# Block-sparse attention and a top-1 expert router on one core: a third of the score mask moves from TensorE to GpSimd, settled rows are divided later, ranks are kept in 16 bits, and 25 expert tiles always run

## The chip, the cores and the metric

The kernel runs on one core of one Trainium2 chip, and the metric is the device time of one execution in microseconds (us). The engines are PE (TensorE, matrix multiply; its weight loads are listed apart as PEld), DVE (VectorE), ACT (ScalarE), POOL (GpSimd) and SP (SyncE, which issues most DMAs). They run side by side and wait for each other through semaphores. SBUF is the on-chip memory, PSUM the memory that PE writes its results to.

## The reference, cut to what matters

```python
# attention: B, H, S, D = 4, 8, 768, 64; blocks of 32 positions
scores = scale * np.matmul(q, k.transpose(0, 1, 3, 2))
mask = np.abs(blk_i - blk_j) <= 1
mask = mask | (blk_i == 0) | (blk_j == 0) | (blk_i == n_blocks - 1) | (blk_j == n_blocks - 1)
for qb in range(n_blocks):
    for kb in sampled_blocks[qb]:                       # 3 random key blocks for each query block
        mask[qb * block:(qb + 1) * block, kb * block:(kb + 1) * block] = True
scores = np.where(mask, scores, -1000000000.0)
attn = np.exp(scores - max); attn = attn / (sum + 1e-9)
out = np.matmul(attn, v)
# (B, H, S, D) -> x: 3072 rows of 512
# router: cosine of each row with 8 expert vectors, softmax, the best expert only
xn = x / (norm(x) + 1e-6); logits = xn @ en.T / tau
expert_idx = argmax(logits); gate_w = probs[expert_idx]
for e in range(8):                                      # w1[e]: 512 x 1024, w2[e]: 1024 x 512
    out[mask_e] = gate_w * (relu(x[mask_e] @ w1[e]) @ w2[e])
```

## The kernel before: the parts concerned

The attention is cut into 192 units, numbered `u`. A unit is one chunk of 128 keys (`kc`, 0 to 5, so `kc = u % 6`) against half of the queries (`HALF` = 384) of a pair of heads. Six units make one window `w` (32 in all), two windows one pair of heads, 48 units one batch. Scores stand with keys on partitions and queries along the row, and no maximum is subtracted: a masked entry gets minus 1e9 added to it before `exp`. That addition is a matmul of its own, in 16 bits, into the same PSUM tile as the scores:

```python
def score_fast(k, u):
    ps = k.big.tile([P, 2, 512], F32, name="sc", tag="big")            # two such PSUM tiles
    ...
    for rows, cols, first in ((k.kmask, k.qmask, True), (kt, qt, False)):
        for h, r, keys in quarters:                                     # 4 quarters of the PE array
            nc.tensor.matmul(ps[D * r:D * (r + 1), h, 0:HALF], lhsT=rows[D * h:D * (h + 1), keys],
                             rhs=cols[D * h:D * (h + 1), queries], start=first, stop=not first)
    e = k.ep.tile([P, 2, HALF], F32, name="e", tag="e")                 # four such tiles
    k.exps = nc.scalar.activation(e, ps[:, :, 0:HALF], ACT.Exp, scale=SCALE)

def attend_fast(k, u):
    if kc == 0:   k.av = k.acc.tile(...); k.first = e                   # one accumulator in PSUM
    elif kc == 1: k.summed = nc.vector.tensor_tensor(out=k.esum, in0=k.first, in1=e, op=ALU.add)
    else:         k.summed = nc.vector.tensor_tensor(out=k.esum, in0=k.esum, in1=e, op=ALU.add)
    for r in range(2):
        for h in range(2):
            nc.tensor.matmul(k.av[...], lhsT=v[...], rhs=e[...], start=(kc == 0), stop=(kc == NC - 1))
    if kc == NC - 1:
        nc.scalar.copy(out=part, in_=k.av[:, 1, 0:HALF])
        k.summed = nc.vector.tensor_tensor(out=at, in0=k.av[:, 0, 0:HALF], in1=part, op=ALU.add)
```

A window that is complete is settled in the next one: matmuls turn it back to rows with queries on partitions and add up the denominators; DVE divides; GpSimd squares the rows and adds the squares by halving the width, for the norm.

```python
def settle(k, w):
    ... # 12 matmuls "back" (rows), 24 matmuls "back" (sums), into one PSUM tile
    nc.vector.reduce_sum(out=den..., in_=sums, axis=AX.X)
    nc.vector.tensor_scalar(out=den, in0=den, scalar1=1e-9, scalar2=None, op0=ALU.add)
    k.tick = nc.sync.dma_start(out=k.ticks[w:w + 1, :], in_=den[0:1, 0:1])
    nc.vector.reciprocal(...); nc.vector.tensor_tensor(x ...); nc.vector.tensor_tensor(part ...)

def squares(k, w):
    nc.gpsimd.tensor_tensor(out=sq, in0=x, in1=x, op=ALU.mult)          # 128 x 384
    width = P // 2
    while width:                                                        # 192, 96, 48, 24, 12, 6, 3
        k.squared = nc.gpsimd.tensor_tensor(out=..., in0=..., in1=..., op=ALU.add).ins
        width //= 2

# in the loop over units
    if u % NC == 3 and NC < u < units - 2 * NC: settle(n, u // NC - 1)
    if u % NC == 4 and NC < u < units - 2 * NC: squares(n, u // NC - 1)
    ... # routing of the batch before, in steps given by a plan of units
    steps = [partial(attend_fast, n, u)] + ([partial(score_fast, n, u + 2)] if u + 2 < units else [])
    for step in reversed(steps) if u % NC == 0 else steps: step()
    ... # transposes of the next pair's q and k on DVE (two of 128 x 384 in each of four slots)
```

`rank`, once for each of four batches, counts with three fp32 matmuls how many rows before this one chose the same expert. The experts then run in tiles of 128 rows: 5 early tiles (`NE`), then up to 24 late ones (`NL`), of which 19 (`NU`) are sure to be needed. The rest stand each behind a test of the number of tiles in use; after them a last test asks whether all softmax sums were in range, or whether the exact program has to run.

```python
    for i in range(NE + NU):                            # 24 tiles, always
        fetch(n, i); expert_tile(n, i) or mixed_tile(n, i)
    used = n.nc.values_load(n.used[0:1, 0:1], min_val=0, max_val=NL)
    with ExitStack() as more:
        for i in range(NU, NL):                         # up to 5 more, each inside the test before
            more.enter_context(n.tc.If(used > i))
            fetch(n, NE + i); expert_tile(n, NE + i)
...
    fast(n)
    good = n.nc.values_load(n.good[0:1, 0:1], min_val=0, max_val=N * H)
    with tc.If(good < N * H):
        exact(n)
```

With the inputs given, 25 tiles are needed (23 whole ones and two mixed ones appear in the trace): 24 always, one behind a test.

Of the kernel before, what the change touches and what calls it, by code (L numbers as in the profile page):

```python
# [39 lines left out]
         for big in range(E + 1) for low in range(E + 1 - big))  # L40

# [9 lines left out]
NEG = -1.0e9  # L51

# [31 lines left out]
def build_consts(k):  # L84
# [16 lines left out]
    k.before = pool.tile([P, P], F32, name="before")  # L101
# [15 lines left out]
    k.oh = pool.tile([P, NT, E], F32, name="oh")  # L117
    k.rank = pool.tile([P, NT], F32, name="rank")
    k.seen = pool.tile([P, NT + 1, E], F32, name="seen")
# [238 lines left out]
def score_fast(k, u):  # L358
# [7 lines left out]
    for rows, cols, first in ((k.kmask, k.qmask, True), (kt, qt, False)):  # L366
        for h, r, keys in quarters:
            nc.tensor.matmul(ps[D * r:D * (r + 1), h, 0:HALF], lhsT=rows[D * h:D * (h + 1), keys],  # L368
                             rhs=cols[D * h:D * (h + 1), queries], start=first, stop=not first)
    e = k.ep.tile([P, 2, HALF], F32, name="e", tag="e")  # L370
    k.exps = nc.scalar.activation(e, ps[:, :, 0:HALF], ACT.Exp, scale=SCALE)  # L371
    k.es[u] = e

# [26 lines left out]
def settle(k, w):  # L400
# [5 lines left out]
    if w % (2 * NPAIR) == 0:  # L406
        k.x[b] = k.xp.tile([P, NC, ND, XE], F32, name="x", tag="x")
        k.nsq[b] = k.xp.tile([P, NC, NPAIR], F32, name="nsq", tag="nsq")
        k.part[b] = k.xp.tile([P, NC, H, E], F32, name="part", tag="part")
# [10 lines left out]
    for t in range(NQ):  # L420
        for h in range(2):
            for r in range(2):
                for s in range(2):
                    cols = slice(t * P + D * s, t * P + D * (s + 1))
                    nc.tensor.matmul(sums[D * s:D * (s + 1), t, h, r:r + 1], lhsT=esum[D * r:D * (r + 1), h, cols],  # L425
                                     rhs=k.ones[D * r:D * (r + 1), 0:1], start=True, stop=True)
    den = k.dens[:, w, :]
    nc.vector.reduce_sum(out=den.rearrange("p (t h) -> p t h", t=NQ), in_=sums, axis=AX.X)
    nc.vector.tensor_scalar(out=den, in0=den, scalar1=1e-9, scalar2=None, op0=ALU.add)
# [12 lines left out]
def squares(k, w):  # L442

    nc = k.nc
    b, j, qh = w // (2 * NPAIR), w // 2 % NPAIR, w % 2
    chunks = slice(qh * NQ, (qh + 1) * NQ)
    x = k.x[b][:, chunks, j, 0:P]
    sq = k.sp.tile([P, NQ, P], F32, name="sq", tag="sq", bufs=1)
    nc.gpsimd.tensor_tensor(out=sq, in0=x, in1=x, op=ALU.mult)  # L449
    width = P // 2  # L450
    while width:
        out = sq[:, :, 0:width] if width > 1 else k.nsq[b][:, chunks, j:j + 1]
        k.squared = nc.gpsimd.tensor_tensor(out=out, in0=sq[:, :, 0:width], in1=sq[:, :, width:2 * width],  # L453
                                            op=ALU.add).ins
        width //= 2


def last_squares(k, w):

    b, j, qh = w // (2 * NPAIR), w // 2 % NPAIR, w % 2  # L460
    for c in range(qh * NQ, (qh + 1) * NQ):
        sq = k.sp.tile([P, P], F32, name="sq_l", tag="sq_l")
# [4 lines left out]
def count_good(k):  # L467
# [14 lines left out]
    nc.vector.tensor_copy(out=k.good, in_=ps[:, 0:1])  # L482

# [79 lines left out]
def rank(k, b):  # L563
# [5 lines left out]
    nc.tensor.matmul(rk, lhsT=k.before, rhs=oh, start=True, stop=False)  # L569
    nc.tensor.matmul(rk, lhsT=k.ones, rhs=k.seen[:, b * NC:(b + 1) * NC, :], start=False, stop=True)  # L570
    nc.tensor.matmul(ps[:, NC * E:(NC + 1) * E], lhsT=k.ones, rhs=k.seen[:, (b + 1) * NC, :], start=True, stop=True)
# [278 lines left out]
def fetch(k, i):  # L850

    if i + 2 < NE + NL and i + 2 != NE:
        fetch_rows(k, i + 2)
    need = [(t, at) for t in range(NE + NL) for at in parts(t)]
# [6 lines left out]
def prepare(k, i):  # L861
# [14 lines left out]
    with k.tc.issue_after(k.relu):  # L876
# [9 lines left out]
def expert_tile(k, i, meanwhile=None, then=None):  # L886
# [20 lines left out]
    if i + 1 < NE + NL:  # L907
# [18 lines left out]
def mixed_tile(k, i):  # L926
# [21 lines left out]
    for f0, row in zip((0, half), rows):  # L948
# [4 lines left out]
        if f0 == 0 and i + 1 < NE + NL:  # L953
# [9 lines left out]
def after_sequence(n, b):  # L963

    routing = partial(next, route(n, b), None)
    plan = [(7, routing), (14, routing), (16, routing), (17, routing), (20, partial(rank, n, b)), (23, routing)]
# [14 lines left out]
def attention_fast(n, ctx):  # L981
# [4 lines left out]
    n.ld, n.tp, n.ep = pool("ld", 3), pool("tp", 2), pool("ep", 4)  # L986
# [28 lines left out]
    plan, experts = [], build_experts(n)  # L1015
    for u in range(units):
# [5 lines left out]
        if u % NC == 4 and NC < u < units - 2 * NC:  # L1022
            squares(n, u // NC - 1)
# [7 lines left out]
        for when, what in plan:  # L1031
            if when == u % (per * NPAIR):
                with n.tc.issue_after(n.summed.ins), n.tc.issue_after(n.exps.ins), n.tc.issue_after(n.tick.ins):
                    what()

        steps = [partial(attend_fast, n, u)] + ([partial(score_fast, n, u + 2)] if u + 2 < units else [])
        for step in reversed(steps) if u % NC == 0 else steps:
            step()
        turn = u % per - (0 if g else NC - 1)
# [7 lines left out]
        if u >= units - 4 and u % 2 == 0:  # L1047
            squares(n, 2 * B * NPAIR - 3 + (u == units - 2))
# [38 lines left out]
def expert_tiles(n, between=(), first=None, then=None, spread=None):  # L1087
# [5 lines left out]
    between, n.scattered = iter(between), None  # L1093
    for i in range(NE + NU):
# [8 lines left out]
        next(between, None)  # L1103
    used = n.nc.values_load(n.used[0:1, 0:1], min_val=0, max_val=NL)
    with ExitStack() as more:
        for i in range(NU, NL):
            more.enter_context(n.tc.If(used > i))
            n.scattered = None
            fetch(n, NE + i)
# [3 lines left out]
def fast(n):  # L1113
    n.rings, n.loads, n.squared = {}, 0, None
    with ExitStack() as ctx:
# [20 lines left out]
        def last_rows():  # L1136
            settle(n, 2 * B * NPAIR - 1)
            last_squares(n, 2 * B * NPAIR - 1)
# [8 lines left out]

def exact(n):
    n.exact, n.rings = True, {}
    with ExitStack() as ctx:  # L1150
# [3 lines left out]
        n.small = pool("small_x", 1, space=PSUM)  # L1154
# [15 lines left out]
        expert_tiles(n)  # L1170


@with_exitstack
def kernel(
# [19 lines left out]

    n.raw, n.turned, n.done, n.part, n.nsq, n.turned_rows = {}, {}, {}, {}, {}, {}
# [8 lines left out]
    good = n.nc.values_load(n.good[0:1, 0:1], min_val=0, max_val=N * H)  # L1204
    with tc.If(good < N * H):
        exact(n)
# [32 lines left out]
```

## Time and profile before

Three runs took 699.25, 699.12 and 698.61 us, median 699.12. The profiled execution has a span of 697.6 us at a granted PE clock of 0.994 of full speed.

| stretch of the span, us | PE busy | DVE busy | ACT busy | POOL busy | DMA share |
|---|---|---|---|---|---|
| 8.00 to 325.00, attention | 316.87 | 252.06 | 167.97 | 168.04 | 0.53 |
| 325.00 to 684.80, expert tiles | 359.28 | 86.78 | 17.82 | 123.91 | 0.95 |
| 684.80 to 697.60, end | 0.00 | 0.73 | 0.00 | 1.01 | 0.06 |

Busy times are sums in us within the stretch. In a list by time, each row gives start, duration, engine, source line, operation, output and inputs. A duration of a matmul includes its way through the array, so neighbouring matmuls overlap; what one costs PE is the distance from its start to the next start. Rows named POOLq, PEq and the like are what an engine's sequencer does (loads of registers, branches, semaphores).

### The profile page before, as it was taken

The page shows a single profiled execution, that of the slowest core. Times are in us where ns is not written, and L with a number is a line of the kernel's source. Part 1 is how long each engine was busy: PE and PEld are TensorE (multiplying, and loading weights), DVE is VectorE, ACT ScalarE, POOL GpSimd, SP SyncE. Part 2 cuts the span into 40 slices and gives each one's busy share as a digit, 9 for nine tenths or more (in the row PEclk, how much of TensorE's full clock was granted, in tenths as well). Part 3 has the DMA queues.
Part 4 walks back from the last instruction along what each step waited for, and adds up shares of the span by engine and source line. Part 5 has one row for each costly group of instructions (what it writes and reads, how often), then busy time and mean ns, then how long its engine had stood idle before and what let it go on. Part 6 is the DMA issues. An engine that isn't in the chain of part 4 may idle for free.

```text
span 697.6 us, 19415 instructions
## 1 busy us (share of the span) xinstructions
PE 682.9 (98%) x8237; PEld 453.5 (65%) x8237; DVE 344.4 (49%) x733; ACT 188.4 (27%) x266; POOL 295.6 (42%) x450
## 2 busy tenths in 40 slices
PE   9999999999999999999999999999999999999992
PEld 4677777555555557557767677666576755667770
DVE  6887778777788888765671111211121111211120
ACT  5555555555555555553100000000100000000000
POOL 1355466544774468545402244323342243323430
PEclk9999999999999999999999999999999999999997
DMA  7733444575226769652999889998899998999990
GB/s 123 130 62 50 55 70 70 130 145 118 55 43 161 138 160 195 222 172 94 341 406 369 339 303 341 357 350 302 297 409 403 405 372 310 420 390 419 359 342 25
DMA packets 172650, 164.87 MB, mean 236 GB/s; under 512 B 129340, under 2 KB 129340, under 8 KB 169478
## 3 DMA queue, kind: packets, MB, share of 16 engines
q1 hardware_dynamic: 165734, 149.86, 68.0%
q0 software_dynamic: 5216, 13.43, 5.3%
q8 instruction: 68, 1.11, 0.7%
q10 hardware_dynamic: 1600, 0.20, 0.2%
q14 instruction: 32, 0.26, 0.1%
HBM read 147.66 MB, written 16.07 MB: 235 GB/s over the span
## 4 chain that ended last, share of the span: by engine, by line
PE 96%; DMA 1%; issue 1%; DVE 0%; POOL 0%; ACT 0%; POOLq 0%
PE hp L896 23%; PE sc L368 22%; PE yp L911 22%; PE av L390 18%; PE back L425 3%; PE hp L939 2%; PE yp L959 2%; PE back L418 2%; DMA out_dram<-y,slot_l 1%; PE warm L81 1%; PE xg_ps L872 0%; DVE row L945 0%; PE hp L951 0%; PE rk L569 0%; POOL out_dram L920 0%
## 5 line engine op out<-in xcount | busy, mean ns | idle before, releaser
L371 ACT ACTIVATE e<-sc 128x768 f32<-128x768 f32 x192 | 155.5, 810 | 149.6 <-PE sc L368 147.7
L896 PEld LDWEIGHTS hp<-xgt,w 128*128 128x128 f32 x1472 | 167.8, 192 | 10.8 <-issue 10.2
L896 PE MATMUL hp<-xgt,w 128*128 128x128 f32 x1472 | 169.3, 275 | 0.0
L368 PE MATMUL sc<-qt,kt 64*64 64x384 f32 x1536 | 164.4, 482 | 0.0
L911 PE MATMUL yp<-w,h 128*128 128x512 f32 x368 | 161.7, 592 | 0.0
L390 PE MATMUL av<-e,vld 64*64 64x384 f32 x1536 | 160.7, 486 | 0.0
L387 DVE TENSOR_TENSOR esum<-esum,e 128x768 f32<-128x768 f32 x128 | 128.8, 1006 | 34.7 <-ACT e L371 30.9
L911 PEld LDWEIGHTS yp<-w,h 128*128 128x128 f32 x368 | 68.2, 190 | 77.0 <-issue 76.5
L453 POOL TENSOR_TENSOR sq<-sq 128x192 f32<-128x192 f32 (+1 forms) x186 | 101.8, 547 | 13.9
L817 POOL DMA_INDIRECT xg<-x_dram,quarter x88 | 88.3, 1004 | 32.9 <-issue 27.7
L390 PEld LDWEIGHTS av<-e,vld 64*64 64x64 f32 x1536 | 64.1, 133 | 46.0 <-issue 17.4
L899 ACT ACTIVATE h<-hp 128x512 f32<-128x512 f32 x23 | 13.7, 597 | 291.4 <-PE hp L896 291.4
L368 PEld LDWEIGHTS sc<-qt,kt 64*64 64x64 f32 x1536 | 66.9, 133 | 31.3 <-issue 23.2
L920 POOL DMA_INDIRECT out_dram<-y,slot_l x20 | 20.1, 1007 | 156.4 <-DVE y L919 151.1
L903 DVE TENSOR_SCALAR h<-hp 128x512 f32<-128x512 f32 x23 | 15.9, 691 | 129.4 <-PE hp L896 129.4
L449 POOL TENSOR_TENSOR sq<-x 128x384 f32<-128x384 f32 x31 | 28.5, 918 | 116.7 <-DVE part L438 97.9
L368 PE MATMUL sc<-qmask,kmask 64*64 64x384 bf16 x768 | 73.7, 323 | 0.1
L919 DVE TENSOR_SCALAR y<-yp,gate 128x512 f32<-128x512 f32 x20 | 15.0, 751 | 100.9 <-PE yp L911 88.8
L368 PEld LDWEIGHTS <-kmask 64*64 64x64 bf16 x768 | 31.4, 107 | 26.3 <-issue 21.4
L385 DVE TENSOR_TENSOR esum<-e 128x768 f32<-128x768 f32 x32 | 31.1, 973 | 7.5 <-ACT e L371 7.5
L425 PE MATMUL back<-ones,esum 64*64 64x1 f32 x1536 | 27.5, 191 | 0.0
L425 PEld LDWEIGHTS back<-ones,esum 64*64 64x64 f32 x1536 | 26.7, 135 | 0.0
(204 smaller groups left out, 367.5 us busy)
## 6 DMA issues: line engine op xcount, KB each, us to landing
w<-in_moe_w_dram SPq DMA_DIRECT2D x54, 2048.0 KB
w<-in_moe_w_dram SPq DMA_DIRECT2D x16, 512.0 KB
x_dram<-x SPq DMA_DIRECT2D x24, 258.0 KB
vld<-in_v_dram SPq DMA_DIRECT2D x32, 192.0 KB
kld<-in_k_dram SPq DMA_DIRECT2D x60, 96.0 KB
qld<-in_q_dram SPq DMA_DIRECT2D x60, 96.0 KB
x_early<-x SPq DMA_DIRECT2D x12, 258.0 KB
xg<-x_dram,quarter POOLq DMA_INDIRECT x88, 6.2
```

The source lines that it names most:

```text
L368: nc.tensor.matmul(ps[D * r:D * (r + 1), h, 0:HALF], lhsT=rows[D * h:D * (h + 1), keys], rhs=cols[D * h:D * (h + 1), queries], start=first ...
L371: k.exps = nc.scalar.activation(e, ps[:, :, 0:HALF], ACT.Exp, scale=SCALE)
L385: k.summed = nc.vector.tensor_tensor(out=k.esum, in0=k.first, in1=e, op=ALU.add)
L387: k.summed = nc.vector.tensor_tensor(out=k.esum, in0=k.esum, in1=e, op=ALU.add)
L390: nc.tensor.matmul(k.av[D * h:D * (h + 1), r, 0:HALF], lhsT=v[D * r:D * (r + 1), h, kc, :], rhs=e[D * r:D * (r + 1), h, :], start=(kc == 0 ...
L425: nc.tensor.matmul(sums[D * s:D * (s + 1), t, h, r:r + 1], lhsT=esum[D * r:D * (r + 1), h, cols], rhs=k.ones[D * r:D * (r + 1), 0:1], star ...
L449: nc.gpsimd.tensor_tensor(out=sq, in0=x, in1=x, op=ALU.mult)
L453: k.squared = nc.gpsimd.tensor_tensor(out=out, in0=sq[:, :, 0:width], in1=sq[:, :, width:2 * width], op=ALU.add).ins
L817: k.nc.gpsimd.indirect_dma_start(out=x[:, g], out_offset=None, in_=quarters, in_offset=bass.IndirectOffsetOnAxis(ap=k.quarter[:, g, t:t + ...
L896: nc.tensor.matmul(hp[:, f, :], lhsT=w1[:, d, (f0 + f) * P:(f0 + f + 1) * P], rhs=xt[:, d, :], start=(d == 0), stop=(d == ND - 1))
L911: nc.tensor.matmul(yp, lhsT=h[:, f, :], rhs=w2[:, f, :], start=(f == 0), stop=(f == NF - 1))
L920: k.scattered = nc.gpsimd.indirect_dma_start(out=k.out[:, :], out_offset=bass.IndirectOffsetOnAxis(ap=slot, axis=0), in_=y[:, :], in_offse ...
```

## The change

- **Mask.** In the units with `kc` 1 or 4 (from the second pair of heads on, without the numbers listed in `WHOLE`, counted within a batch) the four mask matmuls are left out. In their place GpSimd multiplies the exponentials by a mask of ones and zeros, kept in 16 bits. 49 of the 192 units are such units. The mask table is built at the start by 2 x 4 matmuls and two activations. Scores run three units ahead rather than two, with five `e` tiles rather than four, so that GpSimd has time between `exp` and `attend`.
- **Division.** `settle` keeps only the matmuls. The DVE part becomes `divide`, issued at `kc` 5 behind the addition `at`; its reduction becomes an addition of 1e-9 and an addition of two columns.
- **Squares.** The squares of rows leave GpSimd: three ACT activations (square with a sum along the row) per window.
- **Ranks.** The one-hot table, the counts and the triangle of ones are kept in 16 bits; three fp32 matmuls become two in 16 bits.
- **Tiles and branch.** 25 tiles always run (`FULL` = 20 late ones); both tests become one (`todo`), and what is rarely needed lies behind it.

The diff, cut to its core:

```diff
+FULL = min(NU + 1, NL)
+AHEAD = 3
+CUT = (1, 4)
+WHOLE = {1: (10, 13, 19), 2: (10, 13, 19), 3: (10, 13, 19, 43, 46)}
 ...
+    k.ones_b = pool.tile([P, P], BF16, name="ones_b")
-    k.before = pool.tile([P, P], F32, name="before")
+    k.before = pool.tile([P, P], BF16, name="before")        # also oh and seen: F32 -> BF16
 ...
 def score_fast(k, u):
-    for rows, cols, first in ((k.kmask, k.qmask, True), (kt, qt, False)):
+    cut = g > 0 and kc in CUT and u % (2 * NC * NPAIR) not in WHOLE.get(g // NPAIR, ())
+    for rows, cols, first in ((k.kmask, k.qmask, True), (kt, qt, False))[int(cut):]:
         ...
     k.exps = nc.scalar.activation(e, ps[:, :, 0:HALF], ACT.Exp, scale=SCALE)
+    if cut:
+        mask = k.cut[:, CUT.index(kc), queries].unsqueeze(1).broadcast_to([P, 2, HALF])
+        k.squared = nc.gpsimd.tensor_tensor(out=e, in0=e, in1=mask, op=ALU.mult).ins
+def build_cut(k, i):                                          # at u = 3 and u = 5
+    ... # 4 matmuls of kmask and qmask into cut_ps
+    nc.scalar.activation(k.cut[:, i]..., ps[:, :, 0:HALF], ACT.Relu, bias=1.0, scale=-10.0 / NEG)
 ...
+def divide(k, w):
-    nc.vector.reduce_sum(out=den..., in_=sums, axis=AX.X)
-    nc.vector.tensor_scalar(out=den, in0=den, scalar1=1e-9, scalar2=None, op0=ALU.add)
+    nc.vector.tensor_scalar(out=per_row, in0=sums[:, :, :, 0], scalar1=1e-9, scalar2=None, op0=ALU.add)
+    nc.vector.tensor_tensor(out=per_row, in0=sums[:, :, :, 1], in1=per_row, op=ALU.add)
     ... # tick, reciprocal, x, part as before
 def squares(k, w):
-    nc.gpsimd.tensor_tensor(out=sq, in0=x, in1=x, op=ALU.mult)  # and seven halvings
+    for c in range(qh * NQ, (qh + 1) * NQ):
+        k.nc.scalar.activation(sq, k.x[b][:, c, j, 0:P], ACT.Square, accum_out=k.nsq[b][:, c, j:j + 1])
 ...
 def rank(k, b):
-    nc.tensor.matmul(rk, lhsT=k.before, rhs=oh, start=True, stop=False)
-    nc.tensor.matmul(rk, lhsT=k.ones, rhs=k.seen[:, b * NC:(b + 1) * NC, :], start=False, stop=True)
-    nc.tensor.matmul(ps[:, NC * E:(NC + 1) * E], lhsT=k.ones, rhs=k.seen[:, (b + 1) * NC, :], start=True, stop=True)
+    nc.tensor.matmul(ps[:, 0:(NC + 1) * E]..., lhsT=k.ones_b,
+                     rhs=k.seen[:, b * NC:(b + 1) * NC + 1, :], start=True, stop=False)
+    nc.tensor.matmul(rk, lhsT=k.before, rhs=oh, start=False, stop=True)
 ...
     # loop over units
-    n.ep = pool("ep", 4)
+    n.ep = pool("ep", 5)
-        if u % NC == 4 and NC < u < units - 2 * NC: squares(n, u // NC - 1)
+        scored = u + (AHEAD if u > NC else 2)
+        steps = [partial(attend_fast, n, u)] + [partial(score_fast, n, i) for i in range(ahead, min(scored + 1, units))]
+        if u % NC == 5 and NC < u < units - 2 * NC:
+            with n.tc.issue_after(n.summed.ins): divide(n, u // NC - 1)
+        if u % NC == 1 and 2 * NC < u < units - NC:
+            with n.tc.issue_after(n.exps.ins): squares(n, u // NC - 2)
 ...
-    for i in range(NE + NU):
+    for i in range(NE + FULL):
 ...
-    good = n.nc.values_load(n.good[0:1, 0:1], min_val=0, max_val=N * H)
-    with tc.If(good < N * H):
-        exact(n)
+    todo = n.nc.values_load(n.todo[0:1, 0:1], min_val=0, max_val=2)
+    with tc.If(todo > 0):
+        more(n)                                               # rare tiles, and the exact program
```

## The prediction

> **What bounds the kernel now.** I read the page's chain first, then the list by time inside the attention, then the end of the span.
>
> ```profile
> PE 96%; DMA 1%; issue 1%; DVE 0%; POOL 0%; ACT 0%; POOLq 0%
> PE hp L896 23%; PE sc L368 22%; PE yp L911 22%; PE av L390 18%; PE back L425 3%; PE hp L939 2%; PE yp L959 2%; PE back L418 2%; DMA out_dram<-y,slot_l 1%; PE warm L81 1%; PE xg_ps L872 0%; DVE row L945 0%; PE hp L951 0%; PE rk L569 0%; POOL out_dram L920 0%
> ```
>
> PE carries 96% of the chain, so only what leaves PE, or starves it, counts. The next view shows two units of the attention. Read the starts.
>
> ```profile
> 203.53 0.82 PE L390 MATMUL av<-e,vld 64*64 64x384 f32 x8
> ...
> 203.83 0.81 ACT L371 ACTIVATE e<-sc 128x768 f32<-128x768 f32 x1 [1.78 <-PE sc L368]
> ...
> 204.17 0.34 PE L368 MATMUL sc<-qmask,kmask 64*64 64x384 bf16 x4
> ...
> 204.27 0.83 POOL L449 TENSOR_TENSOR sq<-x 128x384 f32<-128x384 f32 x1 [2.12 <-DVE x L435]
> 204.33 0.82 PE L368 MATMUL sc<-qt,kt 64*64 64x384 f32 x8
> 204.67 1.23 DVE L387 TENSOR_TENSOR esum<-esum,e 128x768 f32<-128x768 f32 x1 [0.38 <-ACT e L371]
> ...
> 204.98 0.82 PE L390 MATMUL av<-e,vld 64*64 64x384 f32 x8
> ```
>
> One unit is 204.98 - 203.53 = 1.45 us: av 0.64, mask 204.33 - 204.17 = 0.16, scores 0.65. I compared starts through the whole attention: hardly 1 us is lost beyond these costs. PE does not wait. Between two sections PE settles a window in 1.04 us (201.00 to 202.04 in the same list). In the expert tiles the chain repeats 7.14 + 6.87 = 14.01 us a tile, without a gap either.
>
> The end is the other stretch where something can be won:
>
> ```profile
> 685.81 1.01 POOL L920 DMA_INDIRECT out_dram<-y,slot_l  x1 [5.34 <-DVEq L1105]
> ```
>
> ```profile
> L1204 POOLq TENSOR_LOAD <-good x1: 303/303/303, 689.9 to 689.9; - x1
> ```
>
> ```profile
> L1205 POOLq COMPARE_BRANCH x1: 50/50/50, 690.3 to 690.3; - x1
> L1205 POOLq INC_SWDGE_SEM x1: 410/410/410, 695.3 to 695.3; - x1
> ```
>
> The last scatter is issued at 685.81. GpSimd waits until it has landed (3.2 us), leaves the nested tests, loads `good` at 689.9 and branches at 690.3; 7.3 us later the span ends.
>
> **What the Trainium skill says.** "Trainium Kernel Development and Optimization", section Performance Expectations, calls matmul busy time a bad metric because matmuls are pipelined. The trace agrees: the mask row is listed with 73.7 us busy for 192 units, 0.38 us each, while start to start it costs 0.16. The change can win the second figure, not the first. "GPSIMD Engine Reference", section 3.1, gives 4497 ns for a two-input operation on 2048 fp32 elements; in proportion that is an estimate of 1.69 us for 768. This trace is used instead, below. "SBUF — State Buffer", section on the two separate sides, says that a GpSimd operation and a DVE operation with two SBUF inputs exclude each other for a whole instruction. The trace agrees: the esum above runs into POOL's product and takes 1.23 us against a median of 0.96, and the squares take up to 1.585 us against a median of 0.826.
>
> **The change part by part.**
>
> *Mask matmuls.* Kc 1 and 4 are 64 of 192 units; minus 4 of the first pair and 11 in the lists leaves 49. 49 x 0.16 = 7.8 us off PE. Building the table adds 2 x 0.16 = 0.3 us.
>
> *Masking on GpSimd.* The rows that size it:
>
> ```profile
> L449 POOL TENSOR_TENSOR sq<-x x31: 823/826/1585, 27.0 to 325.9; 128x384 f32<-128x384 f32 x31
> ```
>
> ```profile
> L453 POOL TENSOR_TENSOR nsq<-sq x31: 192/193/974, 32.5 to 329.2; 128x3 f32<-128x3 f32 x31
> ```
>
> Undisturbed, 384 elements take 823 ns and 3 take 192: 1.656 ns an element, so 768 take 192 + 765 x 1.656 = 1459 ns (fp32 operands; I assume that the 16-bit mask costs the same). Is it on the path? Count from the end T of the scores of a kc 1 unit, in starts. Activation begins at T + 0.24 to 0.30 and takes 0.81: e is there at T + 1.05. GpSimd starts 0.09 later and ends at T + 2.6; about 0.25 more to PE's first matmul is T + 2.85. With three units ahead PE does meanwhile av (0.64), scores (0.81), scores (0.81), av (0.64): it comes to this unit at T + 2.90. So kc 1 just fits. Kc 4 has the settling in between too: 3.93 us, over 1 us to spare. With two ahead it would not have fitted.
>
> *Contention.* Before, POOL's squares cost it 28.5 us and 114.5 us (101.8 + 12.7) for 31 windows, 4.6 us a window; now 2 x 1.46 = 2.9. DVE in a window: six-unit sum 5 x 0.96, `at` 0.56, division about 1.1, on average 1.1 of transposes, 7.6 us; a window lasts 6 x 1.45 + 1.04 - 2 x 0.16 = 9.4 us. Walking one window: `at` ends at T + 2.0, the first sum waits for the masked tile (2.6 to 3.6), division to 4.8, second sum to 5.75; the kc 4 mask, ready at 5.3, waits for it and runs to 7.1; three sums end at 9.8; the next `at` is due at 10.9. With four transposes the last sum ends at about 10.5. So a plain window loses nothing, and DVE has only 0.4 us to spare in one with transposes. Where routing and early dispatch add DVE work (43.2 of 50 us busy at 200 to 250 us), it will run late, and a late `at` holds the accumulator. I allow 3 us for this, and 0.5 for the table's two activations in the first units. Both are judgement.
>
> *Squares on ACT.* The three last squares took 0.30 us plus 0.19 for reading the sum: 3 x 0.49 = 1.5 us a window. ACT is at 167.97 of 317 us; 31 x 1.5 = 46 more leaves a third idle. The exponential behind them (kc 5) comes 0.8 us late and is needed 2 us later. Nothing on the path. The freed GpSimd is worth nothing in itself.
>
> *Division.* Some ten DVE operations change places; the pair 0.162 + 0.165 us is replaced by two as small. No gain, as PE did not wait for it; it keeps `at` ahead of waiting work.
>
> *Ranks.* In the last batch the three fp32 matmuls start at 340.97, 341.12 and 341.34, and the next work at 341.55: 0.58 us. Two in 16 bits I put at 0.15. 4 x 0.43 = 1.7 us.
>
> *Tiles and branch.* The 25th tile follows the 24th with no gap on PE already, so running it always wins nothing. The end does: the branch that led to the end stood at 690.3, behind the landing of the scatter. Now the register load and branch follow the scatter's issue directly: 685.81 + 1.01 + 0.3 + 0.1 = 687.2. That is 3.1 us earlier, and I take the 7.3 us behind it as unchanged (the landing, at 689.0, lies within it). Weights fetched for tiles that never run also go; nothing waited for them.
>
> Sum: 699.1 - 7.8 + 0.3 - 1.7 - 3.1 + 3.5 = **690.3 us**, 1.3% less.
>
> **The rivals.**
>
> 1. *The masked tile becomes the wait.* If a 16-bit or broadcast operand makes the multiplication 2.0 us rather than 1.46, kc 1 comes 0.5 us late in about 25 windows, and the gain falls to nothing: 699 to 703 us. For it: the slack of 0.05 us, and that the two engines exclude each other. Against: the lists of exceptions look fitted to the slots where GpSimd has routing work, and kc 4 has room.
> 2. *DVE becomes the bound.* Each mask may hold a sum for up to 1.3 us. If a window with transposes ran over by 0.5 us, in 16 windows, 8 us would go: 695 us. For it: 0.4 us of slack. Against: POOL's total falls from 4.6 to 2.9 us a window.
> 3. *Full gain, nothing lost.* 699.1 - 12.3 = 687 us. For it: the walk of the plain window has no stall. Even so it is under 2%.
> 4. *The end isn't shortened,* because the wait for the landing, not the branch, sets it: 693 us.
>
> **Range and chances.** Rival 3 with a little more from the end gives the low end, 686; rival 1 at moderate size the high end, 698. Faster by over 2% needs 685.1 us, 14 us less, when all that I can find on PE and in the end is 12.3: 5%. Slower by over 2% needs 713, some 0.5 us of stall in every cut unit over the whole gain: 3%.
>
> **What would show it.** PE's start-to-start time of a cut unit should be 1.29 us against 1.45, and the mask matmuls should fall from 768 to 572 (plus 8 for the table). The multiplication should show 49 times with a minimum near 1.46 us. PE's waits by releaser should stay within a few us in sum; a large wait of av on POOL proves rival 1, one on `at` rival 2. Rank should show two matmuls within 0.2 us. From the last scatter's issue to the span's end should be 8.7 us against 11.8. The prediction is wrong if the multiplication takes 2 us or more, if the attention ends later than about 321 us from the start (325.0 before; 319.7 by this sum), or if the end keeps its length.

## The result and the profile after

| | median us | runs | lowest to highest | profiled span, us |
|---|---|---|---|---|
| kernel before | 698.99 | 6 | 698.61 to 699.25 | 697.6 |
| changed kernel | 704.25 | 6 | 703.48 to 705.17 | 702.6 |

The change makes the kernel slower by 0.75%: the ratio is 1.0075 (95% interval 1.0062 to 1.0088). 690.3 us was predicted, and 698 was the upper end of the range. I cut both spans at the same instructions: the first q·k matmul, the first `hp` of the expert tiles, the end of the last matmul, the end of the span.

| stretch, us | before | after | difference | predicted difference |
|---|---|---|---|---|
| first q·k to first `hp` (attention) | 317.65 | 319.33 | +1.7 | -5.3 |
| first `hp` to the end of the last matmul | 359.70 | 359.17 | -0.5 | -0.4 |
| issue of the last scatter to the end of the span | 11.78 | 15.93 | +4.1 | -3.1 |

The predicted -5.3 is -7.8 + 0.3 + 3.5 and three of the four ranks (-1.3); the fourth lies in the expert tiles. Two stretches went wrong by 7 us each, and 690.3 + 7 + 7 is what was measured. The granted PE clock was 1.00 from 8 to 318 us in both kernels, so the attention was not slowed by it.

The page of the changed kernel gives the chain of waits: first the shares of the engines, then of the lines.

```profile
PE 86%; DVE 7%; issue 1%; ACT 1%; DMA 1%; POOL 1%; POOLq 0%; DVEq 0%; ACTq 0%
PE hp L929 24%; PE yp L944 22%; PE sc L378 16%; PE av L419 14%; DVE esum L416 3%; PE back L450 3%; PE yp L992 2%; PE hp L972 2%; PE back L443 2%; POOL e L384 1%; ACT e L381 1%; DVE qt L294 1%; DVE esum L414 1%; DMA kld<-in_k_dram 0%; DVE nrm L559 0%
```

Before, PE had 96% of this chain and DVE 0%. Now 7% runs over DVE, and the lines named are those of the attention: `esum`, `qt`, `nrm`. The two lines `sc` and `av` have fallen from 40% to 30%, though the attention is no shorter. The groups by cost of the same page show the multiplication (busy us, mean ns; then the idle time before it):

```profile
L416 DVE TENSOR_TENSOR esum<-esum,e 128x768 f32<-128x768 f32 x128 | 144.6, 1130 | 13.4 <-POOL e L384 3.8
L384 POOL TENSOR_TENSOR e<-e,cut 128x768 f32<-128x768 f32 x49 | 90.4, 1846 | 155.5 <-ACT e L381 155.5
```

Its own instructions, listed by tile, with minimum, median and maximum in ns:

```profile
L384 POOL TENSOR_TENSOR e<-e,cut x49: 1640/1654/2446, 29.1 to 312.1; 128x768 f32<-128x768 f32 x49
```

The minimum is 1640 ns, not 1459. The same view for the sums, first of the kernel before, then of the changed one:

```profile
L387 DVE TENSOR_TENSOR esum<-esum,e x128: 912/958/1595, 11.1 to 323.7; 128x768 f32<-128x768 f32 x128
```

```profile
L416 DVE TENSOR_TENSOR esum<-esum,e x128: 911/958/2399, 10.8 to 324.5; 128x768 f32<-128x768 f32 x128
```

Minimum and median stayed; the maximum rose from 1.6 to 2.4 us. A sum itself takes what it took before, but some stand behind a multiplication: in the trace 17 of them start within one, and each ends 0.81 to 0.82 us behind its end, so it waits the multiplication out in full. What PE waits for is in the view of the waits (total us, times, longest), first before, then after:

```profile
PEld av L390 <- ACT e L371: 10.1, 52, 0.5
PEld av L390 <- DVE at L396: 9.1, 30, 0.4
```

```profile
PEld av L419 <- DVE at L425: 15.1, 28, 2.4
PEld av L419 <- POOL e L384: 12.4, 27, 0.8
...
PE av L419 <- DVE at L425: 4.4, 6, 1.7
```

Not all of these totals is lost, since a weight load that waits is partly hidden behind the matmul before it. The longest waits count: for `at` they grew from 0.4 to 2.4 us, and 1.7 us reached the matmul itself. The list by time shows how that one came about:

```profile
251.35 0.82 PE L419 MATMUL av<-e,vld 64*64 64x384 f32 x8
...
252.64 0.82 PE L419 MATMUL av<-e,vld 64*64 64x384 f32 x8
...
252.95 3.35 DVE L416 TENSOR_TENSOR esum<-esum,e 128x768 f32<-128x768 f32 x2
...
253.59 0.47 ACT L423 COPY part<-av 128x384 f32<-128x384 f32 x1
...
253.84 1.65 POOL L384 TENSOR_TENSOR e<-e,cut 128x768 f32<-128x768 f32 x1 [3.62 <-ACT e L381]
...
256.22 0.55 DVE L425 TENSOR_TENSOR at<-av,part 128x384 f32<-128x384 f32 x1
...
256.82 1.52 PE L419 MATMUL av<-e,vld 64*64 64x384 f32 x16 [1.74 <-DVE at L425]
```

First read the cut unit: 252.64 - 251.35 = 1.29 us, as predicted. Then the stall. `part` is there at 253.59 + 0.47 = 254.06, so `at` could run. But DVE still has two sums to do, late from dispatch work, and between them GpSimd takes the multiplication at 253.84: two sums that need 1.9 us take 3.35. `at` starts at 256.22, over 2 us late; only then is the accumulator free, and PE has stood still for 1.74 us.

At the end, the last scatter by time, and then GpSimd's branch with the release of its transfers' semaphores (ns, start):

```profile
686.69 0.97 POOL L953 DMA_INDIRECT out_dram<-y,slot_l  x1 [13.02 <-DVE y L952]
```

```profile
L1274 POOLq COMPARE_BRANCH  x1: 53/53/53, 687.0 to 687.0; - x1
L1274 POOLq INC_SWDGE_SEM  x1: 2388/2388/2388, 690.3 to 690.3; - x1
```

The branch does come right behind the scatter (687.0), as predicted. But the release takes 2388 ns where it took 410, and in the raw records a DRAIN of GpSimd's follows it with 9.06 us where it took 1.05 (two of at most 0.11 us come after it; below, "last DRAIN" means this long one). These two are 10 us more than before.

### The profile page after: what moved, and what is told of

Its sections match the earlier page's. It is cut to its first block, busy times and chain, and to the rows that moved or that the text cites. A ratio compares the mean times of both kernels' runs of the same rounds, so it can differ in the third digit from the quotient of the medians.

```text
span 702.6 us, 18943 instructions
## 1 busy us (share of the span) xinstructions
PE 676.6 (96%) x8033; PEld 427.1 (61%) x8033; DVE 359.8 (51%) x734; ACT 213.7 (30%) x454; POOL 242.5 (35%) x243
## 3 DMA queue, kind: packets, MB, share of 16 engines
q8 instruction: 65, 1.06, 0.6%
## 4 chain that ended last, share of the span: by engine, by line
PE 86%; DVE 7%; issue 1%; ACT 1%; DMA 1%; POOL 1%; POOLq 0%; DVEq 0%; ACTq 0%
PE hp L929 24%; PE yp L944 22%; PE sc L378 16%; PE av L419 14%; DVE esum L416 3%; PE back L450 3%; PE yp L992 2%; PE hp L972 2%; PE back L443 2%; POOL e L384 1%; ACT e L381 1%; DVE qt L294 1%; DVE esum L414 1%; DMA kld<-in_k_dram 0%; DVE nrm L559 0%
## 5 line engine op out<-in xcount | busy, mean ns | idle before, releaser
L378 PE MATMUL sc<-qt,kt 64*64 64x384 f32 x1536 | 162.1, 482 | 1.4 <-issue 0.8
L416 DVE TENSOR_TENSOR esum<-esum,e 128x768 f32<-128x768 f32 x128 | 144.6, 1130 | 13.4 <-POOL e L384 3.8
L384 POOL TENSOR_TENSOR e<-e,cut 128x768 f32<-128x768 f32 x49 | 90.4, 1846 | 155.5 <-ACT e L381 155.5
L419 PEld LDWEIGHTS av<-e,vld 64*64 64x64 f32 x1536 | 56.6, 133 | 60.1 <-issue 25.9
L850 POOL DMA_INDIRECT xg<-x_dram,quarter x80 | 80.2, 1003 | 28.1 <-issue 22.9
L378 PEld LDWEIGHTS sc<-qt,kt 64*64 64x64 f32 x1536 | 62.6, 133 | 44.0 <-issue 37.9
L378 PE MATMUL sc<-qmask,kmask 64*64 64x384 bf16 x572 | 51.9, 323 | 0.1
L378 PEld LDWEIGHTS <-kmask 64*64 64x64 bf16 x572 | 20.3, 107 | 23.5 <-issue 20.1
L425 DVE TENSOR_TENSOR at<-av,part 128x384 f32<-128x384 f32 x32 | 17.8, 556 | 26.2 <-ACT part L423 26.1
L488 ACT ACTIVATE sq<-x 128x128 f32<-128x128 f32 x96 | 28.3, 299 | 7.2 <-DVE x L476 7.2
```

Source lines behind the costliest of these rows:

```text
L384: k.squared = nc.gpsimd.tensor_tensor(out=e, in0=e, in1=mask, op=ALU.mult).ins
L419: nc.tensor.matmul(k.av[D * h:D * (h + 1), r, 0:HALF], lhsT=v[D * r:D * (r + 1), h, kc, :], rhs=e[D * r:D * (r + 1), h, :], start=(kc == 0 ...
L488: k.nc.scalar.activation(sq, k.x[b][:, c, j, 0:P], ACT.Square, accum_out=k.nsq[b][:, c, j:j + 1])
L850: k.nc.gpsimd.indirect_dma_start(out=x[:, g], out_offset=None, in_=quarters, in_offset=bass.IndirectOffsetOnAxis(ap=k.quarter[:, g, t:t + ...
```

## The experiments

My theory after this reading: the attention lost its gain because the multiplication shuts DVE out, and the end lost its own through something in the form of the branch. Rivals: in the attention, that the masked tile itself comes late; at the end, that the number or the time of GpSimd's transfers decides. "Attention" below is always first q·k to first `hp`, and "end" the last scatter's issue to the end of the span. All ratios are against the kernel before in the same series.

### What the multiplication costs

**e1_no_mask_op** leaves the multiplication out, with nothing in its place:

```diff
-        k.squared = nc.gpsimd.tensor_tensor(out=e, in0=e, in1=mask, op=ALU.mult).ins
+        k.squared = k.exps.ins
```

**e2_mask_aside** lets GpSimd do it, but into a tile of its own that nobody reads, so nobody waits for it:

```diff
+        k.aside = k.ep.tile([P, 2, HALF], BF16, name="aside", tag="aside", bufs=1)
-        k.squared = nc.gpsimd.tensor_tensor(out=e, in0=e, in1=mask, op=ALU.mult).ins
+        k.squared = nc.gpsimd.tensor_tensor(out=k.aside, in0=e, in1=mask, op=ALU.mult).ins
```

Both leave the mask out in 49 units. Rows then go to other experts and further tiles run, so the whole times (721.91 and 727.51 us) cannot be compared with the other kernels; the attention can.

> The changed kernel without GpSimd's multiplication in the 49 cut units (the mask is left out there, so the output is not the reference's). Both theories of the lost attention time (tiles that PE waits for, or DVE held by GpSimd) expect PE's waits to go: the attention should end at about 317 us from the start rather than 326.5, and the whole near 694.5 us, since the end of the span keeps its 16 us from the last scatter. If the attention ends at 323 us or later, neither the wait nor the sharing is the cause, and the new order of scores, division and squares is.

> As the changed kernel, but GpSimd writes the product to a tile of its own (16 bits) that nobody reads; it still reads e behind the exponential, at the same moments. No one waits for the masked tile any more, but GpSimd still holds what it shares with DVE for as long. If DVE held by GpSimd is the cause: most of the loss stays, 700 to 704 us, sums still at 2.2 us where they meet a multiplication. If the wait for the masked tile is the cause: the time falls to that of the kernel without the multiplication, near 694.5 us.

The multiplication aside takes what it took in place (1642 ns at the least). Attention: 311.32 us without the multiplication, 316.59 with it aside, 319.33 in the changed kernel. So 5.3 us come from GpSimd's doing it at all, and 2.7 from waiting for it. The sums, listed by tile, of the kernel without it and of the one with it aside:

```profile
L416 DVE TENSOR_TENSOR esum<-esum,e x128: 911/958/1164, 10.6 to 316.3; 128x768 f32<-128x768 f32 x128
```

```profile
L417 DVE TENSOR_TENSOR esum<-esum,e x128: 914/958/2406, 11.2 to 322.2; 128x768 f32<-128x768 f32 x128
```

The maximum is 1164 ns without and 2406 with, although nothing depends on the product in either. That is the two engines excluding each other, not a dependence. It reaches PE through `at`, as the waits show, in the same order:

```profile
PEld av L419 <- DVE at L425: 9.4, 29, 0.9
```

```profile
PEld av L420 <- DVE at L426: 16.1, 29, 2.4
```

**e5_mask_on_pe** puts the mask back on PE everywhere (`CUT = ()`, no table) and keeps ranks, squares, division and the lead of three, with the end of the kernel before (shown at e3_old_end).

> The changed kernel with the end of the kernel before, and with the mask back on PE in all units (no table, no multiplication); division, squares on ACT, three scores ahead and 16-bit ranks stay. From the run without the multiplication: attention ends at 318.2 + 49 x 0.16 - 0.3 = 325.7 us, whole about 697.8. If the other parts cost nothing by themselves and only the ranks act, it ends at 325.0 - 1.3 = 323.7 us, whole about 695.8. If they are what slowed the attention, it ends at 328 or later.

695.94 us, ratio 0.9953 (0.9937 to 0.997); attention 316.12. Against 317.65 before, the rest of the change wins 1.5 us there. From 316.12 the matmuls left out should lead to 316.12 - 7.8 + 0.3 = 308.6. The changed kernel loses 319.33 - 308.6 = 10.7 us of that: 2.7 even without a multiplication (e1), 5.3 through DVE, 2.7 through the wait. What the first 2.7 are is not settled in full: some 1.3 of it is one gap on PE near 280 us for which the records show no releaser (the changed kernel has one of 1.2 at 287), and 0.6 is a wait for `at` at 18 us, which e1, e2, e8 and the changed kernel have shortly after the two tables are built (13 us), and e5, without tables, has not. The prediction had put 0.5 on that.

**e9_split** makes the multiplication in two halves of 384, so that DVE can come in between:

```diff
+        for h in range(2):
+            k.squared = nc.gpsimd.tensor_tensor(out=e[:, h], in0=e[:, h],
+                                                in1=k.cut[:, CUT.index(kc), queries], op=ALU.mult).ins
```

> The changed kernel with the end of the kernel before, and the multiplication in two halves of 384 elements, between which DVE can get in. If DVE held for the length of one multiplication is what counts, the sums are held for 0.8 us at most, and the attention ends 1 to 3 us earlier than with the old end alone (326.4): whole 695.5 to 697.5. If the wait for the masked tile counts more, the second start (0.2 us) makes each first-kind unit later: 25 x 0.2 = 5 us more, 703 us.

703.88 us, ratio 1.0066 (1.0049 to 1.0083), though it has the old end: attention 324.38, 5 us longer than with one piece (e3: 319.31). The two halves in the list by tile, and who waits for them:

```profile
L385 POOL TENSOR_TENSOR e<-e,cut x98: 906/921/1710, 29.1 to 317.7; 128x384 f32<-128x384 f32 x98
...
  DVE esum L418: 16.0, 18
  DVE esum L416: 9.4, 11
```

The longest sum falls to 1676 ns, but two halves need 1.81 us, and DVE comes in between and makes the product late: DVE now waits 16.0 + 9.4 = 25.4 us for it, against 7.4 + 3.8 = 11.2 in the changed kernel. A shorter hold is no cure if the work gets longer and the product comes later.

**e8_fewer_cuts** takes 17 cuts out of the stretches with routing and dispatch (32 of 49 remain), with the old end:

```diff
-WHOLE = {1: (10, 13, 19), 2: (10, 13, 19), 3: (10, 13, 19, 43, 46)}
+WHOLE = {1: (10, 13, 16, 19, 22), 2: (10, 13, 16) + tuple(range(19, 48, 3)),
+         3: (1, 4, 7, 10, 13, 16, 19, 22, 43, 46)}
```

> The changed kernel with the end of the kernel before, and with 17 of the 49 cut units taken back to PE's mask: those beside routing (16 and 22 in each batch, the first ones of the last batch) and all beside the early dispatch. That costs PE 17 x 0.16 = 2.7 us. If DVE held by GpSimd is what loses time, and loses it where DVE has routing work, some 6 of the 8.7 us of stalls counted there go: attention ends near 323 us, whole about 695 us. If the loss is a wait of every cut unit for its tile, 17 x 0.2 us goes and it stays where the old end alone is, about 698 us.

692.71 us, ratio 0.9907 (0.989 to 0.9923); attention 313.19. PE gets 17 x 0.16 = 2.7 us of matmuls back, and the stretch is still 6.1 us shorter than with 49: the 17 cuts had cost 8.8 us of stalls, half a us each. The waits:

```profile
PEld av L420 <- POOL e L385: 9.9, 21, 0.7
PEld av L420 <- DVE at L426: 9.8, 30, 0.9
```

The longest wait for `at` is 0.9 us against 2.4, and the total is close to that of the kernel before (9.1). Yet 15 sums still wait out a multiplication, against 17 in the changed kernel; what is gone are nine held operations of routing and dispatch. So a hold costs PE time where DVE has no slack to take it up.

**e10_kc4_only** keeps of these 32 only the 15 with `kc` 4 (`CUT = (4,)`), where the multiplication has over 1 us to spare.

> The version with fewer cuts and the end of the kernel before, with only the second kind of unit (kc 4, which has the settling ahead of it) masked by GpSimd: 15 units rather than 32, one table rather than two. PE takes 17 x 0.16 - 0.16 = 2.6 us more for the masks. If each kc 1 unit loses what it wins by waiting for its tile and by holding sums, the attention ends where it did (320.5 us, whole 692.7); if they still win in the calm windows, it ends at about 322.5 us, whole 694.5 us.

696.82 us, ratio 0.9965 (0.995 to 0.9979), attention 314.85 against 313.19 in e8. So the 17 cuts at `kc` 1 do win 1.7 of the 17 x 0.16 - 0.16 = 2.6 us that their matmuls, less one table, come to. It is not `kc` 1 as such that loses, but the stretches where DVE is full.

### What the end costs

**e3_old_end** is the changed kernel with the end of the kernel before: nested tests, and rows and weights fetched for tiles that never run.

```diff
-    between, n.scattered, n.stop = iter(between), None, NE + FULL
-    for i in range(NE + FULL):
+    between, n.scattered, n.stop = iter(between), None, NE + NL
+    for i in range(NE + NU):
 ... # the rest behind nested tests, and the test of `good`, as before
```

> The changed kernel with the end of the kernel before: 24 tiles always, the 25th behind its test inside nested tests, and a second test for the exact program. If the single branch is what makes the end long (15.9 us from the last scatter to the end of the span, 11.8 before, of which GpSimd's last drain takes 9.06 and 1.05), the end returns to about 11.8 us and the time to about 700.1 us. If the end is long for another reason (how much GpSimd did before, or its queue of transfers), it stays at 15.9 us and 704.2 us.

698.46 us, ratio 0.9995 (0.9988 to 1.0002); end 10.62 us. The new end costs 5.3 us against the old one, which is itself 1.2 us shorter here than in the kernel before: there GpSimd stands for 1.8 us (693.45 to 695.25) ahead of the last release, here it does not, and the records give no cause. With the old end, 49 cuts cannot be told from the kernel before (0.5 us less, and the interval includes 1), and the mask on PE (e5) is 2.5 us faster still.

**e4_no_branch** has no test at all (it leaves out the rare program):

```diff
-    todo = n.nc.values_load(n.todo[0:1, 0:1], min_val=0, max_val=2)
-    with tc.If(todo > 0):
-        more(n)
```

> The changed kernel with no test at all after the last tile; the rare tiles and the exact program are left out, the 25 tiles are not. If a jump over the rare program is what GpSimd's long drain follows, the drain should be near 1 us and the whole near 693 us. If the drain waits for something that runs for a fixed time after the last scatter or after the first release of GpSimd's transfer semaphores, it stays long: span's end 12 to 16 us after the last scatter, 700 to 704 us.

699.08 us, end 10.85. Without a branch there is no release, but GpSimd's DRAIN still lasts until 9.06 us after the scatter has been issued in full. So the long wait isn't the branch's.

**e6_two_branches** has the new end with the two tests one after the other, **e11_small_branch** the new end with a second test that GpSimd takes no part in, **e7_wait_landing** lets GpSimd wait for the landing of the last rows ahead of the test:

```diff
+    y = n.rings["y", (NE + FULL - 1) % 2]
+    n.nc.gpsimd.memset(y[:, 0:1], 0.0)
+    n.nc.sync.dma_start(out=n.ticks[0:1, :], in_=y[0:1, 0:1])
```

> The changed kernel, 25 tiles always, but with two tests one after the other (rare tiles, then the exact program) in place of the one around both. If GpSimd's last drain is long (9.06 us) whenever there are fewer than two joins behind the last scatter, the drain falls to about 1 us and the end to some 10 to 12 us: whole 698 to 700 us. If it is short only where the last tile itself stands inside a test, it stays long: with one more jump, 704 to 709 us.

> The changed kernel with a second, tiny test behind the single one (it would write one word to scratch; no transfer of GpSimd's lies in it). If a second load and branch on GpSimd is what keeps the drain short, it falls to about 1 us: whole 699 to 702 us. If only a second release of GpSimd's transfer semaphores does, the drain stays at 9.06 us and the time grows by the branch: 705 to 708 us.

> The changed kernel with its single branch; ahead of the branch GpSimd clears one column of the last y tile, which makes it wait until the last scatter has been read (some 3.3 us after its issue), and SP writes one word of that tile to scratch so that the clearing stays. If the long drain comes from GpSimd jumping while it is still at work on the scatter, the drain falls to about 1 us and the end, from the last scatter, to 3.4 + 7.3 = 10.7 us: whole about 699 us. If a single branch as such makes the end long, it stays at 15.9 us or grows to 19: 704 to 707 us.

e6: 710.55 us, end 22.33, the releases 2.39 and 2.37 us. e11: 703.52 us, end 15.66, one release of 2.39 us; as GpSimd got no second branch, it does not tell what a small second test costs. e7: 706.72 us, end 18.92, release again 2.39 us although everything had landed. Neither the number of tests nor outstanding data shortens the release. What all of these share is the number of GpSimd's transfers: 110. The kernel before, e3 and all with a short release have 115 or 118. The difference of eight is the row fetches for two tiles that never run, which the change takes away (with four weight fetches that SP issued).

**e12_fetch_on** is the changed kernel with these fetches, **e13_old_end_no_fetch** the old end without them.

```diff
-    between, n.scattered, n.stop = iter(between), None, NE + FULL
+    between, n.scattered, n.stop = iter(between), None, NE + NL
```

(In the rare program the old weights are dropped and the limit is set after its fetches.)

> The changed kernel with its single test and 25 tiles always, but rows and weights are fetched on for the tiles that come after, as the kernel before does (eight more row fetches by GpSimd). If what GpSimd has fetched last is what keeps its release and drain short (0.42 and 1.05 us rather than 2.39 and 9.06), they are short here and the whole is 704.2 - 10 = 694 to 696 us, unless the landing holds it (697). If the place of the last tile inside a test is what matters, they stay 2.39 and 9.06 and the whole at 704 to 706 us.

> The changed kernel with the tests of the kernel before (the last tile behind its own test, two joins), but without fetching rows and weights beyond that tile. The mirror of the run with the fetches: if the fetches matter, release and drain are long (2.39 and 9.06 us) and the whole is 698.5 + 10 = 708 us; if the place of the last tile inside a test matters, they stay short and the whole is 698.5 us.

e12: **694.37 us**, ratio 0.9932 (0.9915 to 0.9948), end 6.37. e13: 711.34 us, ratio 1.0172 (1.0155 to 1.0189), end 22.50. The branch and the release of e12:

```profile
L1275 POOLq COMPARE_BRANCH  x1: 53/53/53, 686.6 to 686.6; - x1
L1275 POOLq INC_SWDGE_SEM  x1: 428/428/428, 689.8 to 689.8; - x1
```

Same branch as in the changed kernel, right behind the scatter; only the eight row fetches (and the four weight fetches) are back, and the release is 428 ns. This crosses the two suspects: fetches short, no fetches long, with either form of tests.

**e15_early_fetches**, **e16_one_fetch** and **e17_fetch_more** ask whether closeness to the end or the number counts. They fetch the rows of two tiles, one tile, and two tiles (on top of e12) twice, in the middle of the loop:

```diff
+        if NE <= i < NE + 2:          # e16: i == NE
+            fetch_rows(k, i + 2)
```

> The changed kernel with its single branch at the end and no fetch beyond the last tile, but the rows of two tiles in the middle of the loop fetched twice, so that GpSimd issues as many transfers as when it fetches for two tiles that never run. If the number of GpSimd's transfers decides how long it takes to release its semaphores at the end, INC_SWDGE_SEM is 0.4 us and the last scatter's issue stands about 6.5 us before the span's end: 694 to 696 us. If it is that row fetches follow closely before the last scatters, INC_SWDGE_SEM stays 2.4 us and the end about 15.9 us: 703.5 to 705.5 us. I hold the second for somewhat more likely (0.6).

> The changed kernel with the rows of one tile in the middle of the loop fetched twice: 114 transfers by GpSimd in place of 110. If the long release falls away step by step with each transfer, INC_SWDGE_SEM takes about 1.4 us, half way between 2.39 (110) and 0.43 (118); if it is a threshold between 110 and 115 (115 transfers gave 0.36 in the two kernels without the mask), 0.3 to 0.5 us or still 2.39 us.

> The single branch with fetches beyond the last tile and in addition the rows of two tiles fetched twice: 126 transfers. If more transfers than about 115 always give the short release, INC_SWDGE_SEM stays at 0.43 us and the time at 694 to 697 us. If it is a place in a ring of 16 (126 = 110 + 16), INC_SWDGE_SEM is 2.39 us again and the time about 704 us. I give the second 0.3.

| run | GpSimd transfers | release, us | last DRAIN, us | end, us | time, us |
|---|---|---|---|---|---|
| after | 110 | 2.388 | 9.06 | 15.93 | 704.25 |
| e16_one_fetch | 114 | 0.348 | 0.73 | 5.45 | 695.62 (one run) |
| e12_fetch_on | 118 | 0.428 | 1.06 | 6.37 | 694.37 |
| e15_early_fetches | 118 | 0.428 | 1.06 | 7.96 | 697.7 |
| e17_fetch_more | 126 | 0.588 | 1.71 | 6.69 | 697.19 (one run) |

The two releases at the ends of the row, of e16 and e17:

```profile
L1276 POOLq INC_SWDGE_SEM  x1: 348/348/348, 692.0 to 692.0; - x1
```

```profile
L1277 POOLq INC_SWDGE_SEM  x1: 588/588/588, 692.3 to 692.3; - x1
```

I had held closeness likelier (0.6), and that fell: e15 has the number without the closeness, and without the weight fetches, and its release is short. Its end is 1.6 us longer than e12's for another reason: ahead of the release GpSimd stands for 2.05 us between two checks of semaphores (691.39 to 693.44), though the last rows had landed at 690.90. That is like the pause in the kernel before, and its cause stays open. The time of e17 is longer than e12's mainly because its expert tiles take 362.05 us against 359.17. From 114 to 126 the release grows by (588 - 348) / 12 = 20 ns for each transfer; (2388 - 348) / 20 gives 102 steps more at 110. The DRAIN gives the same count: (1.71 - 0.73) / 12 = 0.082 us a step, and (9.06 - 0.73) / 0.082 = 102. Two separate durations give 102, which fits one count behind both that grows with each transfer and drops between the 110th and the 114th. In e12 something is seen at that place: the list of GpSimd's work by time around its transfers 113 (the scatter) to 115.

```profile
672.28 1.02 POOL L953 DMA_INDIRECT out_dram<-y,slot_l  x1 [7.75 <-DVE y L952]
675.36 1.03 POOL L850 DMA_INDIRECT xg<-x_dram,quarter  x1 [2.07 <-issue]
676.70 1.00 POOL L850 DMA_INDIRECT xg<-x_dram,quarter  x1 [0.30 <-issue]
```

The 114th starts 2.07 us after the 113th has ended, where 0.30 is usual. In e16 the 114th is the last scatter itself, and its issue comes 2.54 us after the last matmul instead of 1.07 (which the end of 5.45 us in the table leaves out). But in e15 and e17 the gap is only 0.5 us, so that this is where the count is cleared remains an inference, as does the count itself; that in these kernels the number of transfers decides is shown.

### Both cures together

**e14_best** has the 32 cuts of e8 and the end of e12.

> 32 multiplications on GpSimd in place of 49, with the single branch and the fetches that go on beyond the last tile. If the two effects add: attention as in the run with 32 multiplications (first hp about 320.5 us), last scatter's issue 6.4 us before the span's end, 694.4 minus 5.7 = 688 to 689.5 us, ratio 0.983 to 0.987 against the kernel before. If the end's gain hangs on where the attention leaves the rest, 690 to 692 us.

688.45 us, ratio **0.9852** (0.9836 to 0.9869); first `hp` at 320.32, end 5.87. The cures add: from 704.25, e8's 5.75 (698.46 - 692.71) and e12's 9.88 lead to 688.6. The chain of waits on its page:

```profile
PE 97%; POOL 1%; ACT 1%; issue 0%; DVE 0%; POOLq 0%; ACTq 0%
```

DVE has left the chain again. This version is faster than both kernels.

## Why the prediction was wrong

- **Mask matmuls, -7.8: right.** 572 remain, and a cut unit takes 1.29 us.
- **Duration of the multiplication, 1459 ns: too small.** It is 1640 undisturbed. I had extrapolated at 1.656 ns an element from a product of a tile with itself and assumed that the 16-bit mask costs the same. With 906 ns for 384 elements (e9) the real rate is (1640 - 906) / 384 = 1.91 ns. The Trainium skill's "GPSIMD Engine Reference", section 3.1, scaled to 768 elements, gave an estimate of 1.69 us, and was nearer; I set it aside for a trace of another operation. With 0.18 us more, the slack of 0.05 us at `kc` 1 is gone, and waiting for the masked tile costs 2.7 us (e2 to the changed kernel). That is rival 1, at about a quarter of its size.
- **The stall allowance of 3.5 us: the first term that failed.** It should have been 10.7. Its largest part, 5.3 us, is rival 2 (put at 8 us): DVE shut out while GpSimd multiplies. I had walked one plain window and found no loss, which holds about there: 32 cuts lose 313.19 - (316.12 - 32 x 0.16 + 0.3) = 1.9 us in all. What I put down to judgement, the stretches with routing and dispatch, was where most of it went: 8.8 of the 10.7. And I counted only operations with two SBUF inputs as excluded. In the changed kernel a DVE operation with one input of 128x6 (`nrm`) takes 1.55 us beside a multiplication, where it takes at most 0.17 in e1:

```profile
109.79 1.65 POOL L384 TENSOR_TENSOR e<-e,cut 128x768 f32<-128x768 f32 x1 [4.28 <-ACT e L381]
...
109.92 1.55 DVE L559 TENSOR_SCALAR nrm<-nrm 128x6 f32<-128x6 f32 x1
```

Not every operation is held: 22 `at`, which read one input from PSUM, start within a multiplication and take their usual 0.55 to 0.56 us. The Trainium skill's "SBUF — State Buffer", section on the two separate sides, names operations in a two-port mode beside those with two SBUF inputs, which would fit `nrm`; the trace shows the hold but not the mode.
- **Ranks, -1.7, squares and division, nothing: right, in sum.** The two rank matmuls start at 119.48 and 119.52, and e5, which has all three with the lead of three units, wins 1.5 us in the attention where three ranks were put at 1.3. None was undone alone.
- **The end, -3.1: the second term that failed, and in its sign.** That a branch directly behind the scatter shortens the end was right, and worth more than I said: 11.78 to 6.37 us in e12. The branch stands 0.34 us behind the scatter's start there, where it stood 4.5 behind; 1.8 of the 5.4 us are the pause of the kernel before. But I took "the 7.3 us behind it as unchanged", named only the weights among the fetches that go ("nothing waited for them"), and did not count the row fetches that GpSimd issues. Taking these away left GpSimd at 110 transfers, and release and last DRAIN grew by 2.0 + 8.0 us. Rival 4 said that the landing would set the end, and put it at no change; e7 shows that the landing is not what made it long.

The two errors together are the whole 14 us. The signs that I had named spoke clearly: the multiplication kept under 2 us at its median, but the attention ended at 326.45 instead of 321 at the latest, and the end did not shrink.

## What to carry to other kernels

Work moved from a saturated engine to an idle one costs the time in which it locks out a third: count that engine's slack in the fullest stretch, not in a plain one, and place the moved work only where there is slack (32 cuts won more than 49). A transfer that nobody needs isn't free to remove: compare the end of the program, release by release, before and after. When two changes share a measurement, undo each alone first; here the long release made a kernel that is 4.6 us faster with the end mended (694.37, 698.99 before) into one that is 5.3 us slower (704.25).

## What the runs showed of the hardware

- In these kernels GpSimd's time at a branch and at the program's end depends on how many indirect transfers it has issued: 0.348 us + 20 ns for each beyond 114 for the release, 0.73 us + 82 ns for the last DRAIN, and 2.39 and 9.06 us at 110. Between 110 and 114 transfers lie 10.4 us. The steps rest on the five kernels of the table; the others with 110 (2.37 to 2.39 us), 115 (0.35 to 0.36) and 118 (0.41 to 0.43) agree.
- An elementwise product on GpSimd of fp32 with a 16-bit mask took 906 ns for 384 elements a partition and 1640 for 768; a tile times itself had taken 823 for 384.
- While GpSimd multiplied, a DVE operation of 0.15 us (`nrm`) took 1.55, and two sums took 3.35 us instead of 1.9. In the changed kernel all 17 sums that start within a multiplication end 0.81 to 0.82 us behind it, while 22 `at` and 22 transposes of `k` take no longer than 0.57 us beside one.
